# Moving one piece of MLP work from behind the attention values to ahead of them

## The chip, the cores and the metric

The kernel runs on one core of one Trainium2 chip. The metric is the device time of one execution in microseconds (us), as the median of several runs. The engines are called by the profile's names: PE (TensorE matmul), PEld (its weight loads), DVE (VectorE), ACT (ScalarE), POOL (GpSimd) and SP (SyncE, which here only issues DMAs).

## The reference

Two blocks follow each other. First comes attention with a threshold: 8 batches, 8 heads, 576 tokens, head size 64. The output goes to rows of tokens, 4608 x 512, and through an MLP with a squared ReLU. All is float32.

```python
scores = scale * np.matmul(q, k.transpose(0, 1, 3, 2))
thresh = np.max(scores, axis=-1, keepdims=True) - tau
scores = np.where(scores >= thresh, scores, -1000000000.0)
scores = scores - np.max(scores, axis=-1, keepdims=True)
attn = np.exp(scores)
attn = attn / (np.sum(attn, axis=-1, keepdims=True) + 1e-09)
x = np.matmul(attn, v)            # then (B,H,S,D) -> (B*S, H*D)
h = x @ w_in                      # 512 -> 2048
r = np.maximum(h, 0.0)
out = (r * r) @ w_out             # 2048 -> 512
```

## The kernel before

**Attention.** Heads are taken in pairs. One pair of heads of one batch is a *visit*; a *step* is one block of 128 query rows of a visit (or the rest of 64 rows, of two visits together). A step has scores on PE (`scores_of_two`, L281, in PSUM banks 0 to 4, two blocks at a time in even steps), their row maxima on DVE (`maxima`, L310), exponents on ACT (L322 to L325), the threshold with the row sum on DVE (`threshold`, L337 to L340) and the division on POOL (`divide`, L345 and L347). The weights are then turned by DVE (`turn_blocks`, L431 to L441) and brought to `wT` by DMAs: most are first set aside in DRAM (`set_aside`, an ACT queue DMA, L408) and read back by SP (`place_blocks`, L449); others go directly (L458, L466).

**Values.** When all blocks of a visit are in `wT`, `values()` (L1052) calls `mix` (L499): 40 matmuls at L502 into PSUM banks 0 and 4, then three copies on ACT (`put`, L485 and L489) into `xT`, a ring of tokens for the MLP. Banks 0 and 4 overlap areas of the scores, so the next scores wait for these copies. Values of a visit come 3 or 4 steps after its last block. After the last of the four pairs of a batch, `values()` also adds to the queue the chunks of 256 tokens that are now complete (`add_chunk`, L881), and enters them in the set `whole`.

**The MLP** works on 18 chunks of 256 tokens. From chunk 2 on each chunk is 28 *pieces*, each 8 or 16 matmuls of about 1.8 us in all: 14 units (`unit`, L644, matmuls at L659) and 14 halves of products (`product`, L749, matmuls at L765). Both layers use seven multiplications in place of eight, so sums and differences have to be made on the side: the token differences T1 to T4 on POOL (`make`, L636), the weight differences on POOL or DVE (`factor_sum`, L590), and the sums of results behind each product (`then`, L782 to L803). Units 5, 6, 7 and 4 take T1, T2, T3 and T4. The order of a chunk's units begins "1 2 5 6 1' 3 7 6' 2' 4", where a prime is the second half. A unit that opens a sum takes a PSUM bank by `keep_bank` (L372) from banks 5, 6 and 7, and gives it back when what reads it has been emitted.

T1 to T3 of a chunk are made at once, in the place of POOL's queue where they are asked for: by unit 1's first half, if nobody asked before, or by a product of the chunk ahead:

```python
if x >= 4 and not half and j + 1 in whole:
    ask((j + 1, "T1"), (j + 1, "T2"), (j + 1, "T3"))
```

This stands in `product`; `x >= 4` are the last three products (6, 7, 3), and `not half` is the first half of one.

**The order of work** is written out by a planner in Python. From the first visit of the paired kind on (step 40) each step is `late_step` (L1024). A step has four quarters, each closed by `fill(quarter)`, which emits pieces as long as the debt `state["left"]` is at least half of PIECE_US (1.76); `rate(s)` sets the quarter so that the queue lasts to the next chunks. The first two quarters come before values, the last two behind. What a piece leaves to do behind it is emitted by `after()`, as a rule during the next piece. In a step with values (`valued`), `at_least(count, made)` (L1020) emits pieces, whatever the debt, until `count` have been emitted since `made`; at the end the debt is cut to a floor of half a piece. After values `place(True)` emits the DMAs that write to `wT` again.

There are 24 valued late steps before the last one (END). Those spoken of below, with the start of their values in the trace of before: step 42 (276.24 us), 57 (398.93), 60 (421.80), 75 (541.44), 78 (563.84), 111 (847.19) and 132 (1029.25). New chunks come in steps 42, 60, 78, 96, 114 and 132.

Of the kernel before, what the change touches and what calls it, by code (L numbers as in the profile page):

```python
# [19 lines left out]
def kernel(  # L20
# [256 lines left out]
    def area(u, odd):  # L277
        at = AT[u, odd][0]
        return big[:, at:at + S].rearrange("p (h k) -> p h k", h=2)

    def scores_of_two(s):  # L281


        vis, i = steps[s]

        def term(u, odd, second_part, lhsT, keys, to=slice(0, P)):
            at, cut = AT[u, odd]
            x0, x1 = (cut, S) if second_part else (0, cut)
            nc.tensor.matmul(big[to, at + x0:at + x1], lhsT, keys[u * D:(u + 1) * D, x0:x1], start=True, stop=True)  # L289

        if i == NBLK:
            for x in range(2):
                for v_ in range(2):
                    for u in range(2):
                        cols = slice(v_ * D, (v_ + 1) * D)
                        term(u, 0, x != u, qmid[u * D:(u + 1) * D, cols], kT[v_], cols)
            return
        for at_, (u, odd, x) in enumerate(((1, 1, 0), (0, 0, 0), (1, 0, 1), (0, 0, 1), (1, 0, 0), (0, 1, 0), (1, 1, 1), (0, 1, 1))):
            at = (i + odd) * P
            term(u, odd, x, qT[u * D:(u + 1) * D, at:at + P], kT[vis % 2])  # L300
            if at_ == 0:
                nc.scalar.copy(seen, big[:, AT[1, 1][0]:AT[1, 1][0] + 1])

    def maxima(s, sc):
        vis, i = steps[s]
        n = len(sc)
        st = stats[s % len(stats)]
        mx = st[:, 0, 0:n]
        for u in range(n):
            nc.vector.tensor_reduce(out=mx[:, u:u + 1], in_=sc[u], axis=AX.XY, op=ALU.max)  # L310
        w = w_slots[(s - first_dma) % (2 if by_dma(vis) else 3)][:, 0:n, :]
        weights[vis, i] = w, sc, st
# [6 lines left out]
    def exponents(vis, i):  # L319
        w, sc, st = weights[vis, i]  # L320
        mx, thr, bias = (st[:, j, 0:len(sc)] for j in range(3))
        nc.scalar.activation(out=bias, in_=mx, func=AF.Copy, scale=-SCALE)  # L322
        nc.scalar.activation(out=thr, in_=mx, func=AF.Identity, bias=ntau8)  # L323
        for u in range(len(sc)):
            nc.scalar.activation(out=w[:, u, :].rearrange("p (h k) -> p h k", h=2), in_=sc[u],  # L325
                                 func=AF.Exp, bias=bias[:, u:u + 1], scale=SCALE)
# [116 lines left out]
    def place_blocks(vis, pair, which=range(4)):  # L443

        wb = blocks[vis, pair]
        if pair < NBLK // 2:
            for j in range(4):
                g0 = (ONE, TWO)[pair] // REST
                nc.sync.dma_start(out=wT[j * 32:j * 32 + 32, g0:g0 + 4, :, :].rearrange("r b c q -> r b (c q)"),  # L449
                                  in_=outside[vis, pair][:, j, :, :])  # L450
            return
        for qb in which:
            rows = slice(qb * 32, qb * 32 + 32)
            for j in range(4):
                to = wT[j * 32:j * 32 + 32, :, :, :]
                at = slice(qb % 2 * 32, qb % 2 * 32 + 32)
                if paired(vis):
                    nc.sync.dma_start(out=to[:, (LEFT if qb < 2 else ODD) // REST, :, at], in_=wb[rows, j:2 * KB:4, :])  # L458
                else:


                    first = j if qb < 2 else KB + (j - KB) % 4
                    n = len(range(first, KB if qb < 2 else 2 * KB, 4))
                    c = first // 4
                    first += 2 if qb < 2 else -KB
                    nc.sync.dma_start(out=to[:, LEFT // REST, c:c + n, at], in_=wb[rows, first:first + 4 * n - 3:4, :])  # L466
# [152 lines left out]
    def some_later(engine):  # L619
        if later[engine]:  # L620
            make(*later[engine].popleft())
# [259 lines left out]
    def add_chunk(j):  # L881
        waiting.extend(pieces_of(j))
        whole.add(j)

    def rate(s):


        if s < out_from:
            return PIECE_US * sum(x[2] == 0 for x in waiting) / (out_from - s)
        have = PIECE_US * len(waiting) - state["left"]  # L890
        best = 1e9
        at = s
        for e in sorted(chunk_at) + [END]:
            if e > s:
                have += sum(other(x) for x in range(at, e))
                at = e
                best = min(best, (have - (RESERVE if e < END else 0)) / (e - s))
                have += PIECE_US * sum(len(pieces_of(x)) for x in chunk_at.get(e, ()))
        return max(best, 0.0) - other(s)
# [7 lines left out]
    def after():  # L907
        now = state["last"]
        state["last"] = []
        for fn in state["then"]:  # L910
            state["last"] += fn() or []
        state["then"] = []
        for fn in now:
            fn()

    def piece():
        _, fn, *what = waiting.popleft()
        state["left"] -= PIECE_US
        state["made"] += 1
        if fn is mlp_out or what[0] <= PLAIN and what[1] == 0:  # L920
            after()
        then = fn(*what)
        after()
        state["then"] = then
        if state["step"] >= NST:
            some_later("vector")
            some_later("gpsimd")

    def fill(us):
        state["left"] += us  # L930
        while waiting and state["left"] >= PIECE_US / 2 and waiting[0][0] <= state["usable"]:
            piece()
        state["left"] = min(state["left"], PIECE_US)
# [75 lines left out]
    def turn_last(s):  # L1009
        if s <= NST:  # L1010
            turn_blocks(*steps[s - 1])
            n, i = steps[s - 1]
            if i % 2 and by_dma(n) and goes_out(n, i // 2):
                set_aside(n, i // 2)

    def goes_out(n, pair):

        return pair < NBLK // 2

    def at_least(count, made):  # L1020
        while waiting and state["made"] < made + count:
            piece()

    def late_step(s):  # L1024

        on = s < NST
        odd = on and steps[s][1] % 2 == 1
        if on:
            n, i = steps[s]
            if not odd:  # L1030
                scores_of_two(s)
            after()
            maxima(s, [area(u, odd) for u in range(2)])
            some_later("gpsimd")
            exponents(n, i)
        first = s > NST or steps[s - 1][1] % 2 == 1 or steps[s - 1][1] == NBLK
        if first:
            turn_last(s)
        valued = s in mixes and s < END

        todo = list(place_at[s])

        def place(all_):
            for what in list(todo):
                if all_ or not goes_out(*what[:2]):
                    place_blocks(*what)
                    todo.remove(what)

        if not valued:
            place(False)  # L1050

        def values():  # L1052
            if s in mixes:
                while (visits[mixes[s][0]][0] // HP + 1) * S - RING > read_to["x"]:
                    piece()
                mix(*mixes[s])
                for j in chunk_at.get(s, ()):
                    add_chunk(j)

        if s == END:  # L1060
            values()
        quarter = rate(s) / 4 if s < END else 1e9
        made = state["made"]
        fill(quarter)
        some_later("gpsimd")
        after()
        if on:
            threshold(n, i)
            divide(n, i)
        if first:  # L1070
            some_later("vector")
        fill(quarter)
        after()
        if not first:
            some_later("vector")
            turn_last(s)
        for fn in prep_at[s] + load_at[s]:
            fn()
        some_later("gpsimd")
        if valued:  # L1080
            at_least(1, made)
            made = state["made"]
            values()
        some_loads()
        place(True)
        some_later("vector")
        some_loads()
        fill(quarter)
        some_loads()
        fill(quarter)  # L1090
        some_loads()
        if valued:
            at_least(2, made)
            state["left"] = max(state["left"], -PIECE_US / 2)

    for s in range(END + 1):
# [142 lines left out]
```

## Time and profile before

| | us |
|---|---|
| median of 3 runs | 1334.75 (1334.66 to 1335.83) |
| profiled execution, its own time | 1334.19 |
| its span, first to last instruction | 1332.4 |
| PE busy | 1297.2 |
| DVE busy | 928.2 |
| POOL busy | 758.3 |
| ACT busy | 585.2 |

The mean granted clock of PE was 0.995 of full speed. A line of a timeline gives the start, the time from the first start to the last end, the engine, the line of the kernel, the operation, what it writes and reads with shapes, and how many instructions were merged; in brackets stands the engine's idle time ahead of it and what ended that. A line of the waits gives the total, the number of times and the longest.

### The profile page before, as it was taken

The numbers are of one execution on the slowest core, as the hardware profiler recorded it, in microseconds if no ns is written. First come the engines' busy times: TensorE is split into PE (matmuls) and PEld (weight loads), VectorE is DVE, ScalarE is ACT, GpSimd is POOL, SyncE is SP. The second block draws the span as 40 slices with busy tenths as digits, with TensorE's granted clock in tenths as the row PEclk, the third lists the DMA queues.
The fourth block names the chain that finished last, engine by engine and source line by source line (L and its number), as shares of the span: only waits on it lengthen the run. The fifth ranks groups of instructions, "written<-read, shape, count | busy, mean of one in ns | idle before, by whom it ended". The sixth has DMA issues, their size and how long they took to land.

```text
span 1332.4 us, 25133 instructions
## 1 busy us (share of the span) xinstructions
PE 1297.2 (97%) x9112; PEld 1078.2 (81%) x9112; DVE 928.2 (70%) x2026; ACT 585.2 (44%) x1357; POOL 758.3 (57%) x865
## 2 busy tenths in 40 slices
PE   7898999999999999999999999999999999999998
PEld 5676556878796979787888888888887888889997
DVE  6877776777787878777786777868687877732131
ACT  4776674235262535343434443444434343422321
POOL 4689875765655555364655554737274737354451
PEclk7999999999999999999999999999999999999999
DMA  8764531647767686867586685758677577430000
GB/s 159 160 152 117 144 91 36 160 93 183 167 177 170 169 195 165 200 141 200 123 186 147 172 192 138 189 108 205 138 181 169 150 180 164 141 91 1 17 17 16
DMA packets 330124, 186.68 MB, mean 140 GB/s; under 512 B 291440, under 2 KB 291472, under 8 KB 323600
## 3 DMA queue, kind: packets, MB, share of 16 engines
q1 hardware_dynamic: 317696, 116.87, 45.0%
q10 hardware_dynamic: 9504, 59.27, 11.2%
q0 software_dynamic: 2800, 8.93, 1.8%
q8 instruction: 72, 1.18, 0.4%
q14 instruction: 52, 0.43, 0.1%
HBM read 109.22 MB, written 68.42 MB: 133 GB/s over the span
## 4 chain that ended last, share of the span: by engine, by line
PE 85%; DVE 5%; ACT 4%; DMA 3%; POOL 2%; issue 1%; SPq 1%; ACTq 0%; DVEq 0%; POOLq 0%
PE big L659 28%; PE big L765 27%; PE big L502 10%; PE big L289 8%; PE big L548 3%; PE big L273 3%; PE big L730 2%; PE big L386 2%; DMA wT<-aside 2%; DVE st L310 1%; DVE w L337 1%; ACT w L325 1%; ACT wT L387 1%; DMA aside<-turned 1%; PE big L266 0%
## 5 line engine op out<-in xcount | busy, mean ns | idle before, releaser
L337 DVE SCALAR_TENSOR_TENSOR w<-big,st,w 128x576 f32<-128x576 f32 x269 | 207.2, 807 | 97.8 <-ACT w L325 97.5
L310 DVE TENSOR_REDUCE st<-big 128x1 f32<-128x576 f32 x288 | 204.3, 748 | 86.2 <-PE big L289 53.5
L347 POOL TENSOR_SCALAR w<-w,st 128x576 f32<-128x576 f32 x269 | 247.4, 929 | 28.0 <-DVE st L340 24.0
L765 PE MATMUL big<-wo,gsum 128*128 128x256 f32 x1088 | 243.8, 382 | 0.0
L345 POOL TENSOR_SCALAR st<-st 128x2 f32<-128x2 f32 (+1 forms) x148 | 36.6, 247 | 358.6 <-DVE w L337 354.2
L765 PEld LDWEIGHTS big<-wo,gsum 128*128 128x128 f32 x1088 | 204.4, 190 | 37.1 <-issue 8.6
L659 PE MATMUL big<-xT,w_in_sb 128*128 128x128 f32 x1536 | 187.3, 277 | 0.8 <-DVE g L671 0.7
L659 PEld LDWEIGHTS big<-xT,w_in_sb 128*128 128x128 f32 x1536 | 178.5, 192 | 9.8 <-issue 7.6
L765 PE MATMUL big<-wo,g 128*128 128x256 f32 x816 | 185.3, 382 | 0.1
L325 ACT ACTIVATE w<-big,st 128x576 f32<-128x576 f32 x269 | 183.8, 734 | 0.2 <-ACT st L323 0.2
L502 PE MATMUL big<-wT,vs 128*64 128x128 f32 (+5 forms) x1700 | 164.8, 355 | 9.7 <-ACT wT L387 4.2
L765 PEld LDWEIGHTS big<-wo,g 128*128 128x128 f32 x816 | 151.6, 190 | 26.1 <-issue 6.5
L502 PEld LDWEIGHTS big<-wT,vs 128*64 128x64 f32 (+1 forms) x1700 | 97.3, 137 | 73.9 <-issue 21.5
L322 ACT ACTIVATE st<-st 128x2 f32<-128x2 f32 (+1 forms) x148 | 30.3, 205 | 263.4 <-DVE st L310 262.2
L671 DVE TENSOR_TENSOR g<-big,g 128x512 f32<-128x512 f32 x96 | 64.8, 677 | 82.3 <-PE big L659 76.4
L289 PE MATMUL big<-kT,qT 64*128 64x320 f32 (+3 forms) x768 | 108.0, 416 | 0.2 <-DVE w L337 0.2
L289 PEld LDWEIGHTS big<-kT,qT 64*128 64x128 f32 x768 | 84.5, 186 | 15.7 <-issue 4.3
L538 POOL TENSOR_TENSOR gsum<-g 128x512 f32<-128x512 f32 x34 | 46.1, 1356 | 81.6 <-ACT g L668 72.1
L667 ACT ACTIVATE g<-g 128x512 f32<-128x512 f32 x96 | 60.3, 628 | 61.0 <-DVE g L671 59.4
L668 ACT ACTIVATE g<-g 128x512 f32<-128x512 f32 x128 | 80.7, 630 | 4.1
L431 DVE STREAM_TRANSPOSE turned<-w 128x512 f32<-128x512 f32 x100 | 70.3, 703 | 3.7 <-DMA aside<-turned 2.6
L437 DVE STREAM_TRANSPOSE turned<-w 128x512 f32<-128x512 f32 x100 | 66.9, 669 | 0.0
(113 smaller groups left out, 1973.2 us busy)
## 6 DMA issues: line engine op xcount, KB each, us to landing
aside<-turned ACTq DMA_DIRECT2D x50, 1152.0 KB, 5.2
wT<-aside SPq DMA_DIRECT2D x200, 288.0 KB, 5.5
vs<-in_v_dram SPq DMA_DIRECT2D x72, 128.0 KB, 4.4
ql<-in_q_dram SPq DMA_DIRECT2D x126, 72.0 KB, 2.9
wo<-in_moe_w_in_dram SPq DMA_DIRECT2D x16, 512.0 KB, 4.8
wo<-in_moe_w_out_dram SPq DMA_DIRECT2D x16, 512.0 KB, 3.7
out_dram<-osb POOLq DMA_DIRECT2D x32, 256.0 KB, 3.3
kl<-in_k_dram SPq DMA_DIRECT2D x113, 72.0 KB, 3.0
```

Of the source, the lines that this page charges most:

```text
L289: nc.tensor.matmul(big[to, at + x0:at + x1], lhsT, keys[u * D:(u + 1) * D, x0:x1], start=True, stop=True)
L310: nc.vector.tensor_reduce(out=mx[:, u:u + 1], in_=sc[u], axis=AX.XY, op=ALU.max)
L325: nc.scalar.activation(out=w[:, u, :].rearrange("p (h k) -> p h k", h=2), in_=sc[u], func=AF.Exp, bias=bias[:, u:u + 1], scale=SCALE)
L337: nc.vector.scalar_tensor_tensor(out=wu, in0=sc[u], scalar=thr[:, u:u + 1], in1=wu, op0=ALU.is_ge, op1=ALU.mult, accum_out=sm[:, u:u + 1])
L347: nc.gpsimd.tensor_scalar(out=w[:, u, :], in0=w[:, u, :], scalar1=z[:, u:u + 1], scalar2=rcp[:, u:u + 1], op0=ALU.add, op1=ALU.mult)
L431: move(wb[:, 0:h, :, :], whole_[:, 0, :, :, :])
L437: move(wb[:, h + 1:, :, :], whole_[:, 1, :, :, :])
L502: nc.tensor.matmul(ps[u * D:(u + 1) * D, :], vs[n % 2][rows, u * (NBLK + 1) + c, :], wT[rows, at // REST:(at + ps.shape[1]) // REST, NBLK ...
L659: nc.tensor.matmul(to[:, f, :], factor(j, p, q, c)[:, f * P:(f + 1) * P], part[:, c, :], start=(p in "125" and f == 0 and c == 0), stop=(p ...
L668: nc.scalar.activation(out=to, in_=to, func=AF.Square)
L671: nc.vector.tensor_tensor(out=x, in0=to, in1=x, op=ALU.add)
L765: nc.tensor.matmul(to, left[:, f, :], wo[:, slot, f, :], start=(f == 0), stop=(f == HF - 1))
```

## The change

The two counts of `at_least` in `late_step` are exchanged. At least two pieces are emitted in the step before the values, where it was one; and at least one behind the values, where it was two.

```diff
         some_later("gpsimd")
         if valued:
-            at_least(1, made)
+            at_least(2, made)
             made = state["made"]
             values()
         some_loads()
...
         fill(quarter)
         some_loads()
         if valued:
-            at_least(2, made)
+            at_least(1, made)
             state["left"] = max(state["left"], -PIECE_US / 2)
```

## The prediction

> **What bounds the kernel now.** I read the page first, then the waits of TensorE (PE), then each engine's timeline around the 24 steps that the edit touches.
>
> ```profile
> span 1332.4 us, 25133 instructions
> PE 1297.2 (97%) x9112; PEld 1078.2 (81%) x9112; DVE 928.2 (70%) x2026; ACT 585.2 (44%) x1357; POOL 758.3 (57%) x865
> ```
>
> PE decides the end. By stretch, PE is busy 899.23 of the 905.00 us from 255 to 1160, which holds the late steps. So a reordering can gain only the few PE gaps there, and every new gap is paid in full. The waits that this edit could shorten are these (total, times, longest):
>
> ```profile
> PE big L502 <- DMA wT<-aside: 2.8, 3, 1.4
> PE big L502 <- DMA wT<-turned: 1.1, 1, 1.1
> ```
>
> L502 is the values product; four of 24 stall on the DMA that brings the turned weights. PE's timeline shows step 78 with a stall and step 75 without:
>
> ```profile
> 541.44 4.79 PE L502 MATMUL big<-wT,vs 128*64 128x320 f32 x40
> 546.16 3.72 PE L765 MATMUL big<-wo,g 128*128 128x256 f32 x16
> 549.81 1.20 PE L289 MATMUL big<-kT,qmid 64*64 64x384 f32 x16
> ...
> 563.84 2.37 PE L502 MATMUL big<-wT,vs 128*64 128x320 f32 x16
> 567.57 2.63 PE L502 MATMUL big<-wT,vs 128*64 128x256 f32 x24 [1.36 <-DMA wT<-aside]
> 570.14 3.72 PE L765 MATMUL big<-wo,gsum 128*128 128x256 f32 x16
> ```
>
> Start to start, values take 4.72 us undisturbed (541.44 to 546.16) and 6.30 here, a loss of 1.58, more than the 1.36 in brackets. Two pieces (3.65 us) follow, then the next scores (L289).
>
> **The Trainium skill.** (1) "TensorE: Matmul & The Clock Gate", section on the array as 16x 32x32: ACT and DVE are strict first-in-first-out, GpSimd (POOL) too per core, and PE pulls only weight loads ahead. The trace agrees: matmuls start in planned order, and DVE's L671 below starts only after the L590 ahead of it. So an operation emitted behind a waiting one waits too. (2) Same page, "What's actually happening": after an idle window of about 3.4 us the array gets half its clock. Here a 3.82 us gap ends at 14.64 us, and from 14.90 to 28.50 the granted clock is 0.50; later it is 1.00. (3) "Perfetto Trace Analysis", Tensor Engine Instruction: a matmul's end is estimated, so I use starts, which also gave 1.58 against 1.36.
>
> **The change, part by part.** The numbers of pieces come from the plan's own arithmetic, which PE's trace confirms. In all 24 valued steps before END exactly one piece stands ahead of values and two behind. With the edit it is two ahead and one behind: after each such step the plan's debt is the same (three pieces, then the same floor), so all other steps keep their pieces. PE's work is unchanged; 24 times one piece (1.73 to 1.88 us) changes places with values (4.72 us).
>
> *Gain: late DMAs.* Values start one piece later relative to their DMAs, whose issue hangs on scores and maxima that don't move. By starts the losses are step 42: 282.81-276.24-4.72 = 1.85; step 57: 404.12-398.93-4.72 = 0.47; step 60: 427.88-421.80-4.72 = 1.36; step 78: 1.58. One piece covers each but step 42's, where about 0.35 stays. Gain 1.5+0.47+1.36+1.58 = 4.9 us.
>
> *Cost: the moved piece's own operands.* It now runs where values began, 4.7 us earlier against DVE, ACT and POOL. I looked in each step for the last operation that it needs. Most end over 1 us ahead of that point. Exceptions: in steps 60 and 78 its left factor (L789, first half) ends 0.11 us ahead, so its weight load can't be pulled forward: 0.25 each, 0.5 in all (0 to 1.2). In step 111 the moved piece is unit 1 second half; of three PSUM banks two are held, and the third is read by L671:
>
> ```profile
> 845.93 1.45 DVE L590 TENSOR_TENSOR gsum<-w_in_sb 128x512 f32<-128x512 f32 x1
> 847.31 0.68 DVE L671 TENSOR_TENSOR g<-big,g 128x512 f32<-128x512 f32 x1
> ```
>
> PE is ready at 847.19, the bank at 847.99: with the restart 1.0 us (0.8 to 1.3).
>
> *Cost: the T differences.* Values also add new chunks to `whole`. A first-half product of the last three asks POOL for the next chunk's T1 to T3 only if that chunk is in `whole`. In steps 42, 60, 78 and 132 the moved piece is such a product; ahead of values it finds the chunk missing and doesn't ask. The asking falls to a later piece, behind other POOL work, while unit 5, the chunk's third piece, needs T1. POOL and PE at step 60 now:
>
> ```profile
> 427.47 1.63 POOL L347 TENSOR_SCALAR w<-w,st 128x576 f32<-128x576 f32 x2 [0.25 <-DVE st L340]
> 429.07 0.73 POOL L636 TENSOR_TENSOR t<-xT 128x256 f32<-128x256 f32 x1
> ...
> 438.85 2.06 POOL L347 TENSOR_SCALAR w<-w,st 128x576 f32<-128x576 f32 x2
> ```
> ```profile
> 431.53 2.21 PE L289 MATMUL big<-kT,qT 64*128 64x256 f32 x16
> 433.67 3.84 PE L659 MATMUL big<-xT,w_in_sb 128*128 128x128 f32 x32
> 437.35 3.74 PE L659 MATMUL big<-t,g 128*128 128x128 f32 x32
> ```
>
> T1 is done at 429.8, long ahead of unit 5 (437.35). After the edit unit 1 asks, in the second quarter of step 61, behind that step's divide (L347), which waits for DVE's threshold. From step 61's scores: two pieces are done at +5.8; threshold ends at +6.5, divide takes 0.25+0.25+1.65, T1 0.75: +9.4. Stall 3.65 (3 to 4.3). Step 78: unit 1 comes in step 79's first quarter, ahead of divide; POOL must first do L797 0.7, L590 twice 2.5, a store 0.6 and L590 1.25 from 572.15, T1 ends at 577.95, unit 5 is due at 578.2: 0.1 (0 to 1). Step 42: the next product asks behind step 43's divide; T1 ends at 294.5, unit 5 due at 294.3: 0.3 (0 to 1.5). Step 132: T1 to T3 (2.2) now follow divide's end at 1046.26 and push L797 (0.7) and unit 5's factors (L590, 2.5) to 1051.75; unit 5 is due at 1050.34: 1.5 with the restart (0.5 to 2.2).
>
> *At nothing: thinner cover behind values.* Their copies on ACT free the areas of the next scores.
>
> ```profile
> 546.30 0.37 ACT L489 COPY xT<-big 128x256 f32<-128x256 f32 x1 [3.40 <-PE big L502]
> 546.57 0.22 ACT L485 COPY xT<-big 128x64 f32<-128x64 f32 x1
> 546.67 0.39 ACT L489 COPY xT<-big 128x256 f32<-128x256 f32 x1
> ```
>
> They end 0.85 us after values (546.2 to 547.06) in every step; scores follow after one piece, at +1.8. Without that, an ACT pair of 1.26 us ahead of the copies would cost 0.3 a step. The moved piece's own ACT work is emitted behind the copies, at most 0.9 us later than now; whoever reads it comes two pieces later. On SP the wT DMAs behind values (place(True)) wait 1.75 us longer, and the queued loads with them; the loads of this step's transposes are issued ahead, and the next values are three steps off.
>
> *Sum.* 4.9 - (0.5+1.0+3.65+0.1+0.3+1.5) = -2.15: slower by 2.15 us. The profiled execution took 1334.19 (span 1332.4), so 1336.35; the median of the runs is 0.56 above it: 1336.9.
>
> **Rivals.** (a) *Only the DMA stalls go*, since POOL makes T early enough: 4.9-1.5 = 3.4 gained, 1331.3. For it: POOL is 57% busy. Against: the order behind divide in step 61. (b) *Slower, by late T in all four chunk changes*: step 61 4.3, 132 2.2, 42 1.5, 78 1.0 with 0.5+1.0 make 10.5, net 5.6, 1340.3; if step 61's idle stretch halves the clock for one window (estimate from the page: 3.4 at half speed), 1342. It decides as soon as the stalls pass 4.9+2.7 = 7.6 us, half a microsecond above my sum, so this side is near. (c) *The cover behind values fails*: 0.3 in 22 steps is 6.6 on top of my sum, 1343.5. The idle ACT ahead of the copies speaks against it. That the edit does nothing is excluded by the plan.
>
> **How the numbers follow.** A measurement tells about 0.2% (2.7 us, 1332.1 to 1337.4) from no change. My forecast 0.62, of it 0.44 within and 0.18 above; (a) 0.09, of it 0.06 faster and 0.03 within; (b) 0.22, (c) 0.07, both slower. So faster 0.06, same 0.47, slower 0.47; the likeliest case gives 1336.9. The costs' ends put my own case at 1335 to 1339.5; to leave out no more than 2 in 10 the range is 1333 to 1341.
>
> **What would show it.** After: no L502 wait on DMA over 0.4 us; L659 big<-t,g waiting some 3.6 us on POOL in step 61 and about 1.5 at step 132's unit 5; L659 waiting 0.9 on DVE L671 in step 111; scores (L289) starting about 1.8 us after values without a gap. I am wrong if unit 5 never waits, or if scores wait on ACT L489.

## The result and the profile after

The changed kernel takes 1343.43 us (median of 4 runs, 1343.1 to 1344.71) against 1335.29 (1334.66 to 1336.18) for the kernel before beside it: a ratio of 1.0066, with a 95% interval of 1.0053 to 1.0079. It is slower by 8.1 us, where 2.15 were forecast, and above the range. The profiled execution took 1343.46; its page has

```profile
span 1341.7 us, 25134 instructions
...
PE 1301.4 (97%) x9112; PEld 1082.1 (81%) x9112; DVE 924.8 (69%) x2026; ACT 583.9 (44%) x1357; POOL 756.1 (56%) x865
```

PE does the same 9112 matmuls. The waits of PE that have to do with the change (total, times, longest), first after:

```profile
PE big L502 <- DMA wT<-aside: 3.8, 3, 2.2
PE big L659 <- POOL t L636: 3.4, 1, 3.4
...
PE big L659 <- POOL g L590: 1.5, 2, 0.7
PE big L659 <- DVE g L671: 1.4, 2, 0.8
```

The last two of them stood before as

```profile
PE big L659 <- POOL g L590: 0.7, 1, 0.7
...
PE big L659 <- DVE g L671: 0.7, 1, 0.7
```

so one wait of each is new. The wait for T1 (`t`) is the forecast one. The first line should have been gone: values still stall on their DMAs, about as long as before (3.8 us against 2.8 and 1.1), but in other steps.

To say where the 8 us lie I set the starts of the scores (L289) in the two traces beside each other; where the difference changes, time was lost or won. Scores of two blocks stand together, so a change can belong to two steps; the table names the one in which the trace shows its cause. The kernel after is 1.5 us late by step 2 already: pairs of its first 16 matmuls at L273 start 0.48 us apart, where before they start 0.24 apart, so step 2 begins at 16.16 and not at 14.64. The clock came up later there (full speed is first recorded at 12.19, before at 8.06), ahead of the first changed step. Then:

| step | forecast | measured | what is seen there after |
|---|---|---|---|
| 42 | -1.5 | -1.76 | the DMA stall is gone |
| 44, for the chunk of 42 | +0.3 | +0.21 | T late |
| 48 | 0 | **+1.62** | values stall 1.40 on wT<-aside, new |
| 57 | -0.47 | -0.47 | stall gone |
| 60 | -1.36+0.25 | -0.81 | stall of 0.19 left |
| 61 | +3.65 | **+5.24** | 3.40 idle before unit 5, then half clock |
| 75 | 0 | **+2.47** | values stall 2.25 on wT<-aside, new |
| 78 | -1.58+0.25 | -1.45 | stall gone |
| 103 | 0 | +0.59 | L659 waits 0.33 for ACT L691 |
| 111 | +1.0 | +1.03 | bank waits for DVE L671, 0.77 |
| 134, for the chunk of 132 | +1.5 | +1.32 | unit 5 waits for its factors, 0.73 |

With -0.16 at step 66 this is 7.8 us; with the 1.5 of the start 9.3, which is what PE's end is later (1337.76 against 1328.50). Step 61, on PE and on POOL:

```profile
434.01 3.84 PE L659 MATMUL big<-xT,w_in_sb 128*128 128x128 f32 x32
441.25 5.47 PE L659 MATMUL big<-t,g 128*128 128x128 f32 x32 [3.40 <-POOL t L636]
446.55 1.95 PE L659 MATMUL big<-xT,w_in_sb 128*128 128x128 f32 x16
```
```profile
438.60 1.91 POOL L347 TENSOR_SCALAR w<-w,st 128x576 f32<-128x576 f32 x2 [0.24 <-DVE st L340]
440.48 0.72 POOL L636 TENSOR_TENSOR t<-xT 128x256 f32<-128x256 f32 x1
```

T1 stands behind divide, as forecast. But unit 5 itself then takes 5.30 us from start to start (441.25 to 446.55), where it took 3.57 before (437.35 to 440.92). The view of stretches gives the clock granted to PE as the third number from the end of a line (PEclk; behind it stand the DMA share and GB/s):

```profile
438.80:442.20 3.40, 0.95 (x8) 0.95 (x9) 2.80 (x5) 0.00 (x0) 3.32 (x5) 1.00 0.64 253
442.30:445.60 3.30, 3.30 (x17) 3.30 (x17) 0.00 (x0) 1.40 (x3) 3.30 (x4) 0.50 0.37 56
445.70:452.00 6.30, 6.30 (x57) 6.18 (x56) 3.94 (x11) 2.86 (x7) 1.95 (x4) 1.00 0.55 110
```

One window at half speed follows the idle time. The stall in step 75, which had none before:

```profile
548.55 2.37 PE L502 MATMUL big<-wT,vs 128*64 128x320 f32 x16
553.18 2.63 PE L502 MATMUL big<-wT,vs 128*64 128x256 f32 x24 [2.25 <-DMA wT<-aside]
```

The DMAs that it waits for, in SP's own timeline (SPq, which shows issues; the second column runs from the start of the first issue to the end of the last), first before, then after:

```profile
530.10 2.27 SPq L201 DMA_DIRECT2D vs<-in_v_dram  x4
...
533.05 1.92 SPq L449 DMA_DIRECT2D wT<-aside  x4
```
```profile
535.79 4.30 SPq L201 DMA_DIRECT2D vs<-in_v_dram  x7
...
540.77 8.91 SPq L449 DMA_DIRECT2D wT<-aside  x4
```

Before, the four issues took 1.92 us. After, they take 8.91: the fourth is issued at 549.38, and what released SP is the landing of ACT's L408 at 549.36. That DMA writes other weights to DRAM; the fourth wT DMA doesn't read them. The built programs tell why SP waits for it. A completion semaphore is a counter that a DMA raises when its data have landed. Each DMA issued by SP or ACT signals one of eight (in the traces 107, 108 and 110 to 115); they are dealt out in turn over both queues (each of the 1042 DMAs takes the one after its predecessor's), and a DMA waits for the one eight places back. That is how this program was built, not how the chip must be used. The Trainium skill ("DMA: Bandwidth & Descriptors", section on the anatomy of one DMA) says that a semaphore wait happens on the issuing sequencer before dispatch; the trace agrees, with SP standing 5.40 us at this issue and everything behind it in its queue.

SP's own order is the same in both programs. But ACT's L408 stands one to four places earlier among SP's DMAs, in 30 of 50 cases. This fits that SP's DMAs behind values come one piece later; by what rule the build orders the two queues was not looked into. So another of SP's DMAs is eight places behind: in step 48 the third wT DMA in place of a kl load, in step 75 the fourth wT DMA in place of a kl load. And one L408 earlier (step 72's), the second of eight value loads (vs) waits in place of the fifth, so seven are left to issue behind it instead of four, as the two lines on vs show.

### The profile page after: what moved, and what is told of

The parts are those of the page before. It is cut to its first block, busy times and chain, and to the rows that moved or that the text cites. A ratio compares the mean times of both kernels' runs of the same rounds, so it can differ in the third digit from the quotient of the medians.

```text
span 1341.7 us, 25134 instructions
## 1 busy us (share of the span) xinstructions
PE 1301.4 (97%) x9112; PEld 1082.1 (81%) x9112; DVE 924.8 (69%) x2026; ACT 583.9 (44%) x1357; POOL 756.1 (56%) x865
## 4 chain that ended last, share of the span: by engine, by line
PE 83%; DVE 5%; ACT 4%; DMA 3%; POOL 2%; issue 1%; SPq 1%; ACTq 0%; DVEq 0%; POOLq 0%
PE big L765 27%; PE big L659 27%; PE big L502 10%; PE big L289 8%; PE big L548 3%; PE big L273 3%; PE big L730 2%; PE big L386 2%; DMA wT<-aside 2%; DVE w L337 1%; DMA aside<-turned 1%; DVE st L310 1%; ACT w L325 1%; ACT wT L387 1%; POOL w L347 1%
## 5 line engine op out<-in xcount | busy, mean ns | idle before, releaser
L659 PE MATMUL big<-xT,w_in_sb 128*128 128x128 f32 x1536 | 187.2, 277 | 1.5 <-DVE g L671 1.4
L659 PEld LDWEIGHTS big<-xT,w_in_sb 128*128 128x128 f32 x1536 | 178.6, 192 | 9.3 <-issue 6.2
L502 PE MATMUL big<-wT,vs 128*64 128x128 f32 (+5 forms) x1700 | 163.9, 354 | 9.6 <-ACT wT L387 4.2
L502 PEld LDWEIGHTS big<-wT,vs 128*64 128x64 f32 (+1 forms) x1700 | 97.9, 137 | 72.4 <-issue 20.7
L671 DVE TENSOR_TENSOR g<-big,g 128x512 f32<-128x512 f32 x96 | 64.8, 677 | 79.8 <-PE big L659 74.3
L289 PE MATMUL big<-kT,qT 64*128 64x320 f32 (+3 forms) x768 | 107.8, 416 | 0.2 <-DVE w L337 0.2
L289 PEld LDWEIGHTS big<-kT,qT 64*128 64x128 f32 x768 | 84.4, 186 | 15.7 <-issue 4.6
L431 DVE STREAM_TRANSPOSE turned<-w 128x512 f32<-128x512 f32 x100 | 70.3, 703 | 1.2 <-DMA aside<-turned 0.8
L659 PE MATMUL big<-t,g 128*128 128x128 f32 x512 | 63.5, 282 | 4.9 <-POOL t L636 3.4
```

What stands on the lines that cost most here:

```text
L431: move(wb[:, 0:h, :, :], whole_[:, 0, :, :, :])
L502: nc.tensor.matmul(ps[u * D:(u + 1) * D, :], vs[n % 2][rows, u * (NBLK + 1) + c, :], wT[rows, at // REST:(at + ps.shape[1]) // REST, NBLK ...
L659: nc.tensor.matmul(to[:, f, :], factor(j, p, q, c)[:, f * P:(f + 1) * P], part[:, c, :], start=(p in "125" and f == 0 and c == 0), stop=(p ...
L671: nc.vector.tensor_tensor(out=x, in0=to, in1=x, op=ALU.add)
```

## The experiments

My theory from here: the loss beyond my forecast is (a) these shared semaphores and (b) the half clock, and the late T costs what I said. The main rival for (a): the values that stall are late because SP's DMAs behind values are later by themselves, or because the transfers are slow. Not all of the runs were made together, so ratios to the kernel before are compared.

**T asked behind values.** In `product` the condition on `whole` becomes a note, which `values()` reads:

```diff
-        if x >= 4 and not half and j + 1 in whole:
-            ask((j + 1, "T1"), (j + 1, "T2"), (j + 1, "T3"))
+        if x >= 4 and not half:
+            state["next"] = j + 1
+            if j + 1 in whole:
+                ask((j + 1, "T1"), (j + 1, "T2"), (j + 1, "T3"))
...
                     add_chunk(j)
+                    if state.get("next") == j:
+                        ask((j, "T1"), (j, "T2"), (j, "T3"))
```

> The changed kernel, and besides T1 to T3 of a new chunk are asked of POOL right behind values when a first-half product of the last three stood ahead of them. Theory (late T, plus stalls on the turned weights that have another cause): the 3.40 us gap before unit 5 in step 61, the half-speed window behind it, the 0.73 us gap at step 132's unit 5 and the 0.2 at step 44 go: 5.2 + 1.3 + 0.2 = 6.7 us less than the 1343.4 of the changed kernel, 1336.7. The stalls of values in steps 48 (1.4) and 75 (2.25) on DMA wT<-aside stay. Rival (POOL is late in step 61 for a reason other than the place where T is asked): the gap before unit 5 stays over 2 us and the time stays at 1342 or more.

Measured: 1339.56, ratio 1.0034 (1.0021 to 1.0047). Unit 5 follows without a gap:

```profile
436.07 3.74 PE L659 MATMUL big<-t,g 128*128 128x128 f32 x32
439.98 2.05 PE L659 MATMUL big<-xT,w_in_sb 128*128 128x128 f32 x16 [0.17 <-DVE g L671]
```

In the trace step 61 gives back 4.85 and the chunk of step 132 1.32, so the cause of both is the place where T is asked. The total is 2.9 above the expected 1336.7. Of this the trace shows 1.8, in other steps that got worse: step 75's stall is 3.07 instead of 2.25 (+0.83), step 79 loses 0.64 and step 103 0.35. The rest is not explained.

**Two L408s on POOL.** DMAs that POOL issues are not in the round of eight.

```diff
-    def set_aside(vis, pair):
+    def set_aside(vis, pair, engine=nc.scalar):
...
-        nc.scalar.dma_start(out=t, in_=turned[:, 0:NB])
+        engine.dma_start(out=t, in_=turned[:, 0:NB])
...
-                set_aside(n, i // 2)
+                set_aside(n, i // 2, nc.gpsimd if s in (47, 74) else nc.scalar)
```

> The changed kernel, but the two writes of the set-aside weights (L408) that come ahead of the stalled values of steps 48 and 75 are issued by POOL instead of ACT. Theory (SP's wT DMA waits for ACT's L408 to land, because the two share a completion semaphore in the round-robin): with L408 out of that round, SP no longer waits there, the stalls of steps 48 and 75 fall from 1.40 and 2.25 us to under 0.3, offsets 1.6 + 2.5 = 4.1 less: 1339.3. Rival (SP comes later only since its DMAs behind values are later, or the transfers are slow): both stalls stay over 1 us, 1343 to 1344. Step 61's gap of 3.4 us stays in both.

Measured: 1338.87, ratio 1.003 (1.0016 to 1.0044). Step 48's stall is gone (its scores-to-scores time is 1.62 shorter), so there the shared semaphore was all of it. Step 75 keeps 1.29 us of stall, on which the theory as I had put it falls short: no semaphore holds SP at its wT DMAs now, but they are issued 3.7 to 6.3 us after scores (before: 1.0 to 2.5), and L408, at 4.9, runs beside them; the last took 8.3 us to land. That the total came near the expected 1339.3 all the same is in part luck: step 75 gave back 0.95 where 2.5 were expected. This trace also shows step 61's gap of 3.40 with no half clock behind it:

```profile
437.70 3.84 PE L659 MATMUL big<-t,g 128*128 128x128 f32 x32 [3.40 <-POOL t L636]
441.38 1.95 PE L659 MATMUL big<-xT,w_in_sb 128*128 128x128 f32 x16
```

Unit 5 takes 3.68 here, from start to start, and 5.30 in the trace shown above, with the same wait: the half clock costs 1.62.

**Both mendings in one kernel.**

> The changed kernel with both mendings: T asked right behind values, and L408 of steps 47 and 74 on POOL. Theory: the two costs add up, 6.7 + 4.1 = 10.8 less than the changed kernel: 1332.6, that is 2.7 us below the kernel before. Rival (one stall only hides another, which shows when the first is gone): 1336 or more, with a new gap of some us.

Measured: 1333.39, ratio 0.9989 (0.998 to 0.9997): within the noise the two mendings add up (the ratio falls by 0.0032 and 0.0036 with each alone, by 0.0077 with both), and with them the changed order is 0.1% faster than the kernel before. The stall of step 75 is 0.75 here.

**The edit in step 42 alone.**

```diff
-            at_least(1, made)
+            at_least(2 if s in (42,) else 1, made)
             made = state["made"]
...
-            at_least(2, made)
+            at_least(1 if s in (42,) else 2, made)
```

> The edit in step 42 alone, the old counts in all other steps. Theory: step 42's values start 1.8 earlier in the sum, step 44 costs 0.2; and since SP's DMAs behind step 42's values come later, the L408s behind them move in the round, and step 48, whose own order is the old one, stalls on wT<-aside by about 3 us (the fourth wT DMA lands 14.7 after scores as in the changed kernel, the second half of values would start at 11.75). Together 1.6 more than before, about 1337. Rival (a step stalls because its own values are late in SP's queue): no stall in step 48, 1333.5.

Measured: 1338.67, ratio 1.0028 (1.0018 to 1.0038). Step 48, six steps on and with its old counts, stalls by 3.44:

```profile
326.74 2.38 PE L502 MATMUL big<-wT,vs 128*64 128x320 f32 x16
332.56 4.31 PE L502 MATMUL big<-wT,vs 128*64 128x256 f32 x24 [3.44 <-DMA wT<-aside]
```
```profile
317.97 10.25 SPq L449 DMA_DIRECT2D wT<-aside  x4
```

The third wT DMA is issued at 327.44, L408 having landed at 327.42. Against the kernel before just three L408s have moved in the round, those of steps 43, 45 and 47, by 4, 3 and 3 places. The rival is out for this step: its own order is untouched. The clock was 0.50 from 332.59 to 336.00, which I hadn't put in the expectation; the step lost 5.34 in all.

**Small DMAs in the kernel before.** The order of the kernel before, and three DMAs of 64 bytes on ACT that only shift the round.

```diff
+    def small_ones(s, count):
+        for _ in range(count if s in (47, 74) else 0):
+            at = next(smalls)
+            nc.scalar.dma_start(out=small[at:at + 1, :], in_=ident[0:1, 0:16])
...
                 set_aside(n, i // 2)
+                small_ones(s, 3)
```

> The kernel before, untouched in its order, with three DMAs of 64 bytes issued by ACT right behind the L408 of steps 47 and 74. They take three places in the round of completion semaphores, so that in steps 48 and 75 the third of the four DMAs wT<-aside waits for L408 to land instead of a later kl load. Theory (the shared semaphore makes the stall): values stall in step 48 by 4 to 6 us and in step 75 by 6 to 8 us, 10 to 14 us more than before, 1345 to 1350 with a half-speed window. Rival (the stall comes from values being later in the SP queue, or from slow transfers): no stall, within 1 us of before.

Measured: 1341.63, ratio 1.0045 (1.0029 to 1.0062). Both stalls appear with no change in the order of values: 2.16 in step 48 and 3.81 in step 75, where SP waits 7.91 for L408's landing. They are smaller than expected, since only the second group of values (24 of 40 matmuls) waited. A stall of 1.60 in step 147 came besides and was not followed up.

The control had the same three DMAs ahead of L408:

> The control of the run above: the same three small DMAs, issued by ACT right ahead of L408 instead of behind it, so that a ql load and no wT DMA waits for L408. Theory: no stall in steps 48 and 75, within 1 us of before. Rival (the small DMAs themselves disturb): a stall here too.

Measured: 1337.98, ratio 1.002 (1.0011 to 1.003), with stalls of 1.04 and 2.42. As a control it failed. The third wT DMA now stood eight places behind the first small DMA, which ACT issued at 536.76, behind its other work; SP waited 2.83 us for those 64 bytes to land at 539.78, and then its wT DMAs ran beside L408. So it shows the same mechanism once more, and doesn't exclude that the small DMAs disturb in themselves.

**What is left of step 75.** First step 74's L408 is issued by ACT behind step 75's values:

```diff
-            if i % 2 and by_dma(n) and goes_out(n, i // 2):
+            if i % 2 and by_dma(n) and goes_out(n, i // 2) and s not in (74,):
                 set_aside(n, i // 2)
...
+        if s in (74,):
+            set_aside(steps[s - 1][0], steps[s - 1][1] // 2)
         some_loads()
         place(True)
```

> The changed kernel, with step 74's L408 alone issued by ACT behind step 75's values instead of with the turning, so that step 75's four wT DMAs neither wait for it nor run beside it. Theory (of step 75's 2.25 us about half is the shared semaphore and the other half, which stayed when POOL issued L408, is L408's traffic beside the wT DMAs): the stall in step 75 goes altogether, 2.5 less than the changed kernel. Rival (what stayed with POOL was POOL's own doing): 1 us or more of it stays. Step 48's stall of 1.4 and step 61's gap stay.

The changed kernel itself was run once more beside it:

> The changed kernel once more, unaltered, as the measure for the two others on this chip: 1343 to 1344.5, and a second trace of it to see whether the half-speed window behind step 61's gap comes each time.

Measured with the late L408: 1341.29 (ratio 1.0046) against 1346.17 (1.0075) for the changed kernel on the same chip. In the trace step 75's values run through, and the step is 2.47 shorter than in the first trace of the changed kernel, as expected:

```profile
548.22 4.79 PE L502 MATMUL big<-wT,vs 128*64 128x320 f32 x40
```

The medians differ by 4.9. Part of that is in the second trace of the changed kernel, where a half-clock window follows step 75's stall (2.76) too; it loses 2.11 more there than the first.

Then the reason why SP was late at step 75: step 72's L408 on POOL as well, on top of both mendings.

```diff
-                set_aside(n, i // 2, nc.gpsimd if s in (47, 74) else nc.scalar)
+                set_aside(n, i // 2, nc.gpsimd if s in (47, 72, 74) else nc.scalar)
```

> The run with both mendings, and besides the L408 of step 72 on POOL as well. In the changed kernel the second of eight value loads of SP waits for this L408 to land (7.7 us, seven loads still behind it); in the kernel before it was the fifth (3.2 us, four behind), and so step 75's wT DMAs are issued 2.8 after scores instead of 1.0 and run beside step 74's L408. Theory (the shared semaphores make all of step 75's stall, by way of this earlier wait): the wT DMAs of step 75 come no later than 1.5 after scores, the 0.75 us that were left of the stall go, 0.7 less than with both mendings, 1332.3 or so. Rival (SP is late at step 75 because its DMAs behind values are later): wT still at 2.5 or more after scores, 0.5 us or more of stall left.

Measured: 1332.28, ratio 0.9978 (0.9971 to 0.9984). Against the run with both mendings (0.998 to 0.9997) the gain is at the edge of the noise; the trace shows it in its place, with step 75 shorter by 0.97:

```profile
539.80 4.79 PE L502 MATMUL big<-wT,vs 128*64 128x320 f32 x40
```

The wT DMAs come 0.5 ahead of scores to 1.2 behind, and no stall is left, though values and SP's DMAs behind them stand as late as the edit puts them. So step 75's stall, too, goes back to the shared semaphores, in two places: step 72's L408 made SP late, and step 74's L408 held the fourth DMA and slowed the others. The trace has a larger gap in step 103 (1.75; 0.87 with both mendings, 0.33 in the changed kernel): DVE stands 2.09 us at L247 for a ql load, and L671 and ACT's L691 come late behind it. Which wait made that load late I did not try.

**All L408s on POOL**, with T asked behind values:

> The edit in all steps, T asked right behind values, and every L408 on POOL, so that SP never waits for one by a shared semaphore. Theory: no stall of values on wT<-aside over 0.5 us in any step, 1331 to 1333. Rival (POOL, which now waits for DVE's turning 48 times, holds up divide or the squares): new gaps on PE behind POOL, 1335 or more.

Measured: 1333.3, ratio 0.9989 (0.9981 to 0.9998). Steps 48 and 75 have no stall and no new gap stands behind POOL, but step 60's stall on wT<-aside, which the edit had cured, is back with 1.41; the expectation of none over 0.5 was wrong there.

**The gap filled.**

```diff
+        if state["step"] == 61 and (p, q) == ("5", 0):
+            for x in range(20):
+                nc.tensor.transpose(to[:, x % 4, :], ident, ident)
         for f in range(4):
```

> The changed kernel with 20 transposes of the identity ahead of unit 5 in step 61, into the bank that unit 5 then overwrites: extra work that the reference doesn't need, to fill most of the 3.4 us in which PE waits for T1. Theory (the gap itself costs 3.4, the half-speed window behind it 1.6 to 1.8 more where it comes): T1 is no earlier, so scores of step 62 come 1.6 to 1.8 earlier than in a run of the changed kernel with that window, and no window of 0.5 stands there; the median is 0.5 to 1.8 below the changed kernel on the same chip. Rival (the half speed has another cause): a window of 0.5 stands there still.

Measured: 1340.39, ratio 1.0034 (1.0021 to 1.0048).

```profile
436.56 2.35 PE L659 MATMUL big<-ident 128*128 128x128 f32 x20
440.13 3.84 PE L662 MATMUL big<-t,g 128*128 128x128 f32 x32 [1.22 <-POOL t L636]
```

T1 comes no earlier, unit 5 runs at full clock, and the step is 1.62 shorter than in the first trace of the changed kernel: the half clock comes from PE's idle time. One trace alone would not prove it, as the run with two L408s on POOL had no half clock behind the whole gap either; the last section adds what all traces show. The median is 5.8 below the changed kernel's on that chip, more than this; step 48's stall was 0.45 in this trace, 0.94 less, and the rest is not explained.

**The edit in four steps**: the new counts in 42, 57, 60 and 78 only, T asked behind values, and step 47's L408 on POOL.

> The edit in only the four steps whose values had stalled on their DMA (42, 57, 60, 78), the old counts in the twenty others, with T asked right behind values and the L408 ahead of step 48 on POOL. Theory: the gains of those steps stay (1.76 + 0.47 + 0.81 + 1.45 = 4.5), nothing of the costs of steps 48, 61, 75, 104, 111 and 132 is left: 1335.3 - 4.5 = 1330.8, below both kernels. Rival (each gain is given back in a later step): within 1 us of 1335.

Measured: 1332.03, ratio 0.9978 (0.9971 to 0.9985), faster than the kernel before by 0.2% and than the changed one by 0.9% (0.9978 over 1.0066). The four gains show in the trace (1.88, 0.48, 1.22 and 1.04), but steps 61 and 79 lose about 0.6 each, in part as gaps of 0.38 and 0.29 on DVE L671; so the kernel gains about 3 us and not 4.5.

## Why the prediction was wrong, point by point

**Right.** The gains: 4.9 less 0.5 for the gsum waits was forecast, 4.5 came, with a little luck: step 42 gave 0.26 more than forecast and step 60 0.30 less. The T differences: 3.65 forecast in step 61, an idle time of 3.40 measured, behind divide as told, and without the half clock a loss of 3.62; 0.3 and 1.5 forecast for the chunks of steps 42 and 132, 0.21 and 1.32 measured; asking T behind values removed the costs of steps 61 and 132. Step 111: 1.0 against 1.03. Rival (a) is out with the 3.40 in step 61. Rival (c) is refuted, though its 1343.5 is the number nearest to the measured one: ACT's copies end 0.84 to 0.90 us after values, scores start at 1.85 to 1.91, and no step has a gap there.

**The step that failed** is in the part "At nothing": "On SP the wT DMAs behind values wait 1.75 us longer, and the queued loads with them; the loads of this step's transposes are issued ahead, and the next values are three steps off." I costed this at nothing, and it cost 1.62 in step 48 and 2.47 in step 75, with a half-clock window on top in some runs. I asked whether the moved DMAs come in time for their own readers, and they do. What I did not ask is what else their place decides: it moved L408 in the round of semaphores that SP and ACT share, and with that the DMA of SP that stands still until 1152 KB have landed. The part on the gain has the same hole: it lets the issue of the wT DMAs hang on "scores and maxima that don't move", and it hung on the round as well. SP's own waits in the kernel before had the sign of it, in their first line:

```profile
SPq L201 <- DMA aside<-turned: 165.4, 24, 9.7
```

L201 issues loads of inputs, which don't read `aside`. I had these waits ahead of the prediction and did not ask why a load would wait for such a DMA. Of what the prediction named as its signs, "no L502 wait on DMA over 0.4 us" is the one that failed outright; neither of the two under "I am wrong if" came.

**The term that was mis-sized** is step 61: the mechanism and the stall were right, but the half clock behind it, 1.62, stood only in rival (b), as an estimate, and not in my sum. With it and the two stalls the sum of -2.15 becomes 2.15 + 1.6 + 1.6 + 2.5 = 7.9 us slower; 7.8 were measured from the first changed step on. Step 103's 0.59 was not foreseen either; smaller ones the other way, such as those in steps 42, 66 and 134, make up for it. (1334.19 + 2.15 in the sum is 1336.34, not 1336.35; nothing hangs on it.)

**Rival (b)** named "late T in all four chunk changes" with the half clock and 1342. It was near in time for another reason: steps 42 and 78 lost next to nothing to T.

## What to carry to other kernels

Before moving work past DMA issues, look at the waits of the issuing queue itself: where a load waits for a DMA whose data it doesn't read, the two share a semaphore, and any reordering deals these waits out anew, also in steps that it doesn't touch. Here it helped to take single large writes out of that round by issuing them from another queue; with all of them moved one stall came back, so each has to be looked at in its place. The Trainium skill asks for one semaphore per in-flight slot, not one per stream ("DMA: Bandwidth & Descriptors", section on why a DMA increments its semaphore by 16), there so that no data are read before they have landed; that a semaphore handed on from DMA to DMA costs time is what these runs add. A queue that asks for work under a condition (here `j + 1 in whole`) must be followed through each change of order, since an early piece can find the condition not yet met.

## What the runs showed of the hardware

In these traces the half clock did not need a window that was idle throughout. The Trainium skill ("TensorE: Matmul & The Clock Gate", "What's actually happening") tells of free-running windows of 3413 ns and of a cold clock after at least one idle window of about 3.4 us. On the first the traces agree: the clock records step in multiples of 3.413 us. On the second the measurements differ, and they decide. Gaps of 2.24 us (the run with the gap filled, in step 75) and 2.42 us (the control) halved the clock for the next window, while 3.40 us in step 61 (the run with two L408s on POOL) did not. Laying each trace's windows over its gaps, from 30 us on: windows idle for 61% or more were followed by half speed, those idle up to 56% were not, and of two at 59% one was. (A window already at half speed kept it for one more when 41% idle, in step 61 of the run with the late L408.) The gap of 3.40 that did no harm was cut by a window's edge into 1.90 and 1.50. So from 30 us on the border lay between 1.9 and 2.1 us of idle time within one window (56% and 61% of 3.413; PE's ends are modelled, so the shares are estimates). It isn't the whole rule: in the first 30 us four full-speed windows with only 50 to 57% idle were followed by half speed as well, and why stays open. The changed kernel itself shows what the border does: step 75's stall left 49% of a window idle in its first trace, without half speed, and 61% in its second, with it, and the second lost 2.11 us more there, though the stall was just 0.51 longer.
